# One head of an output projection loaded by three DMA engines, and the last value tile loaded in two halves

## The chip, the cores and the metric

The kernel runs on one core of a Trainium2 chip. The metric is the device time of one execution in microseconds (us). A kernel was run several times, and its median is quoted. The experiments were sent in four calls. Each call ran on one chip, with its own runs of the kernel before on that chip; different calls had different chips.

## The reference

Decode attention for 32 sequences with one query each: 32 query heads share 8 key/value heads of 128 elements, and only the last 512 cache positions count. Then comes a projection with wo.

```python
W = min(4096, max(256, Sk // 4))                                # 512
q = (x @ wq).reshape(B, Sq, Hq, Dh).transpose(0, 2, 1, 3)
k = jnp.repeat(k_cache[:, :, Sk - W:, :], rep, axis=1)
v = jnp.repeat(v_cache[:, :, Sk - W:, :], rep, axis=1)
p = softmax(jnp.einsum("bhqd,bhkd->bhqk", q, k) * Dh ** -0.5)
o = jnp.einsum("bhqk,bhkd->bhqd", p, v)
return o.transpose(0, 2, 1, 3).reshape(B, Sq, Hq * Dh) @ wo     # wo: 4096 x 512
```

## The kernel before

All loads but the 32 KB of x go out on one queue, issued by SyncE: keys and values in 2 MB tiles (128 partitions, 16 KB each), wq, and at the end wo. The last value tile, V15, is one load. Then wo follows in eight head groups of 512 KB (128 partitions with rows of 4 KB); the last group is split into 3 KB and 1 KB per partition, so that only a quarter of it has to be waited for last.

```python
# SyncE: the values, then wo
sp.dma_start(V_sb[:, n % NV:n % NV + k].rearrange("p a r d -> p (a r d)"), cache_rows(v_cache, n, k)
).then_inc(sem_v[n % NV], 16)
...
sp.wait_ge(pe_PV, 2 * Z_HOME.rindex("w") + 2)
for hg in range(NHG):
    for i0, i1 in ((0, 4),) if hg < NHG - 1 else ((0, WO_CUT), (WO_CUT, 4)):
        sp.dma_start(
            wo_sb[:, hg, i0:i1].rearrange("p i n -> p (i n)"),
            wo[hg * 512:(hg + 1) * 512, :].rearrange("(m i) n -> m (i n)", i=4)[:, i0 * 512:i1 * 512],
        ).then_inc(sem_last if i0 else sem_wo[hg], 16)
```

TensorE multiplies each value tile in 64 matmuls. Then it reorders the attention output with a band matrix (`select`: partition m of group g must hold rows 4m to 4m + 3 of wo's group), and projects.

```python
def pv(m):                       # waits for sem_v, then 64 matmuls into O_ps
    ...
for hg in range(NHG):
    pe.wait_ge(sem_wo[hg], 16)
    for i in range(4):
        if hg == NHG - 1 and i == WO_CUT:
            pe.wait_ge(sem_last, 16)
        for c in range(2):
            ins = pe.matmul(X_ps[32 * c:32 * (c + 1), 2, 0:256], lhsT=o_sel[:, i, hg, :],
                            rhs=wo_sb[:, hg, i, c * 256:(c + 1) * 256], ...)
ins.then_inc(pe_fin, 1)
```

Of the kernel before, what the change touches and what calls it, by code (L numbers as in the profile page):

```python
# [12 lines left out]
def bass_standalone__sliding_block_cached__sampling_kernel(  # L13
# [32 lines left out]
    WO_CUT = 3  # L46
# [25 lines left out]
    with ExitStack() as es:  # L72
# [13 lines left out]
        mask = sb("mask", [P, NBG], F32)  # L86
        oT_sb = sb("oT_sb", [P, HQ, B], BF16)
# [9 lines left out]
        o_sel = K_0[:, 0:HQ * B].rearrange("p (i g b) -> p i g b", i=4, g=NHG)  # L97
        band = K_0[:, HQ * B:HQ * B + 4 * 224].rearrange("p (i n) -> p i n", i=4)
# [24 lines left out]
        sem_wo = [sem(f"sem_wo{i}") for i in range(NHG)]  # L123
        sem_last = sem("sem_last")
# [33 lines left out]
        pool_qbd = sem("pool_qbd")  # L158
        nc.scalar.dma_start(x_sb, x.rearrange("b s d -> b (s d)")).then_inc(sem_x, 16)
# [27 lines left out]

        def cache_rows(cache, m, k=1):
            q, e = divmod(m, 2)
            rows = cache[4 * q:4 * q + 4, :, SK - W:, :].rearrange("b g (s r) d -> (b g) s (r d)", s=KS)  # L190
            return rows[:, :, e * CR * DH:(e + k) * CR * DH]

        @block.sync
        def _(sp):
            for name in DMA_ORDER:
# [5 lines left out]
                elif name[0] == "K":  # L201
                    if n >= NK:
                        sp.wait_ge(dve_T, 2 * (n - NK + 1))
                    sp.dma_start(
                        K_sb[:, n % NK].rearrange("p r d -> p (r d)"), cache_rows(k_cache, n)
                    ).then_inc(sem_k[n % NK], 16)
                else:
                    k = 2 if n in V_PAIRED else 1
                    if n + k > NV:
                        sp.wait_ge(pe_PV, n - NV + k)  # L210
                    sp.dma_start(
                        V_sb[:, n % NV:n % NV + k].rearrange("p a r d -> p (a r d)"), cache_rows(v_cache, n, k)
                    ).then_inc(sem_v[n % NV], 16)
            sp.wait_ge(pe_PV, 2 * Z_HOME.rindex("w") + 2)
            for hg in range(NHG):
                for i0, i1 in ((0, 4),) if hg < NHG - 1 else ((0, WO_CUT), (WO_CUT, 4)):
                    sp.dma_start(  # L217
                        wo_sb[:, hg, i0:i1].rearrange("p i n -> p (i n)"),
                        wo[hg * 512:(hg + 1) * 512, :].rearrange("(m i) n -> m (i n)", i=4)[:, i0 * 512:i1 * 512],
                    ).then_inc(sem_last if i0 else sem_wo[hg], 16)  # L220
# [8 lines left out]
        def _(pool):  # L229
# [48 lines left out]
            pool.wait_ge(pool_band, 1)  # L278
# [3 lines left out]
            ).then_inc(pool_band, 1)  # L282

        @block.tensor
        def _(pe):
# [64 lines left out]
            def pv(m):  # L350
# [9 lines left out]
                for r in range(CR):  # L360
                    ins = pe.matmul(  # L361
# [7 lines left out]
            def select(b0, b1, dst):  # L369
# [3 lines left out]
                for i in range(4):  # L373
                    for hi in range(4):
# [3 lines left out]
                            rhs=oT_sb[:, :, b0:b1].rearrange("p (g hi) b -> p hi g b", hi=4)[:, hi],  # L378
                            start=(hi == 0), stop=(hi == 3), tile_position=(0, 0), skip_group_check=True,
                        )  # L380
                ins.then_inc(pe_sel, 1)

            for name in PE_ORDER:
                k = int(name[1:])
                {"S": scores, "P": p_turn, "V": pv}[name[0]](k)
                if name == "V12":
                    pe.wait_ge(pool_band, 2)
                    nb = SELCUT
                    select(0, nb, lambda i: X_ps[:, i // 2, (i % 2) * NHG * nb:(i % 2 + 1) * NHG * nb])
            nl = B - SELCUT  # L390
            select(SELCUT, B, lambda i: S_ps[:, i // 2, (i % 2) * NHG * nl:(i % 2 + 1) * NHG * nl])
            pe.wait_ge(dve_sel, 2)
            pe.wait_ge(act_sel, 2)
            for hg in range(NHG):
                pe.wait_ge(sem_wo[hg], 16)
                for i in range(4):
                    if hg == NHG - 1 and i == WO_CUT:
                        pe.wait_ge(sem_last, 16)
                    for c in range(2):
                        ins = pe.matmul(  # L400
                            X_ps[32 * c:32 * (c + 1), 2, 0:256],
                            lhsT=o_sel[:, i, hg, :],
                            rhs=wo_sb[:, hg, i, c * 256:(c + 1) * 256],
                            start=(hg == 0 and i == 0), stop=(hg == NHG - 1 and i == 3),
                            tile_position=(0, 32 * c),
                        )
# [3 lines left out]
        def _(dve):  # L410
# [62 lines left out]
            def sel_evac(src, i0, ni, b0, b1):  # L473
                return (
                    o_sel[:, i0:i0 + ni, :, b0:b1],
                    src[:, 0:ni * NHG * (b1 - b0)].rearrange("p (i g b) -> p i g b", i=ni, g=NHG),
# [3 lines left out]
            dve.tensor_copy(*sel_evac(X_ps[:, 0], 0, 2, 0, SELCUT)).then_inc(dve_sel, 1)  # L480
            dve.wait_ge(pe_PV, NCH)
# [5 lines left out]
            dve.tensor_copy(*sel_evac(S_ps[:, 0], 0, 2, SELCUT, B)).then_inc(dve_sel, 1)  # L487
            dve.wait_ge(pe_fin, 1)
# [3 lines left out]
        def _(act):  # L492
# [52 lines left out]
            for name in ACT_ORDER:  # L545
                arg = [int(a) for a in name[1:].split(".")]
                {"E": soften, "N": norm, "C": pt_evac, "O": o_evac, "Z": spread}[name[0]](*arg)
                if name == "Z7.3":
                    act.wait_ge(pe_sel, 1)
                    act.activation(  # L550
                        o_sel[:, 2:4, :, 0:SELCUT],
                        X_ps[:, 1, 0:2 * NHG * SELCUT].rearrange("p (i g b) -> p i g b", i=2, g=NHG),
                        ACTF.Copy,
                    ).then_inc(act_sel, 1)
            nl = B - SELCUT
            act.wait_ge(pe_sel, 2)
            act.activation(
                o_sel[:, 2:4, :, SELCUT:B],
                S_ps[:, 1, 0:2 * NHG * nl].rearrange("p (i g b) -> p i g b", i=2, g=NHG),
                ACTF.Copy,  # L560
            ).then_inc(act_sel, 1)
            act.wait_ge(pe_fin, 1)
# [29 lines left out]
```

## Time and profile before

| What | Before |
|---|---|
| time, median of the first 3 runs | 187.25 us |
| DMA queue, share of 16 engines over the span | 96.5% |
| last increment of V15's load, slowest engine | 172.57 us |
| first projection matmul | 178.41 us |
| last increment of the last wo load, slowest engine | 182.72 us |
| last matmul ends | 183.06 us |

Times inside an execution count from the start of its span. An "increment" is one of the updates that the records show on a load's semaphore as it lands. In the profile before, each load of the queue got sixteen, and I read each as one DMA engine's share having landed: over the wo loads the sixteen keep their spacing (from the first to the last 3.40 us at group 0 and 3.42 at group 6). So their times show how far the engines lie apart. They and the single packets (start, length, bytes) are records of the trace; the packets do not carry the number of their engine.

### The profile page before, as it was taken

Reading aid. Unit: us, or ns where it says so; the run is one execution under the profiler, and the core shown is the slowest. Engines: PE = TensorE matmul, PEld = TensorE weight load, DVE = VectorE, ACT = ScalarE, POOL = GpSimd, SP = SyncE. Lnnn points to the kernel's source line nnn. Section 1 sums busy time; section 2 is a strip of 40 time slices with the busy share of each in tenths; the row PEclk is TensorE's granted clock in tenths of the full one; section 3 lists DMA queues with packets and bytes.
Section 4 is the critical chain, followed back from the end, with each engine's and each line's share of the span. In section 5 each row is a group of like instructions: output and inputs, shape, how many; then the busy total and the mean of one; then the engine's idle time right before and its main releaser. Section 6 shows DMA issues by size and latency. Waiting matters only on the chain.

```text
span 185.5 us, 3711 instructions
## 1 busy us (share of the span) xinstructions
PE 109.5 (59%) x1540; PEld 90.3 (49%) x1540; DVE 132.1 (71%) x239; ACT 81.2 (44%) x141; POOL 31.8 (17%) x82
## 2 busy tenths in 40 slices
PE   0220303454469704994430899155999989998773
PEld 0100001141369403974130878014998888997761
DVE  0018699979799799979999269999999975510020
ACT  3000100129900686027941005965939999961000
POOL 7100029515300250042330015000003000000000
PEclk9999999999559965799965599755599999999999
DMA  6999999989999999999999999989999999999980
GB/s 201 428 445 424 431 421 484 445 367 424 424 421 445 413 435 421 428 435 410 458 438 392 445 410 442 463 382 442 415 431 431 410 438 417 438 410 416 400 338 30
DMA packets 5872, 75.80 MB, mean 409 GB/s; under 512 B 672, under 2 KB 864, under 8 KB 1888
## 3 DMA queue, kind: packets, MB, share of 16 engines
q1 hardware_dynamic: 5808, 75.53, 96.5%
q8 instruction: 12, 0.20, 0.4%
q10 hardware_dynamic: 48, 0.03, 0.1%
q14 instruction: 4, 0.03, 0.0%
HBM read 75.53 MB, written 0.03 MB: 407 GB/s over the span
## 4 chain that ended last, share of the span: by engine, by line
DMA 41%; PE 22%; DVE 20%; ACT 7%; issue 6%; SPq 3%
PE O_ps L361 16%; DMA V_sb<-in_v_cache_dram 11%; DMA w_sb<-in_wo_dram 11%; DVE KT_sb L439 10%; DMA K_sb<-in_k_cache_dram 10%; DMA w_sb<-in_wq_dram 9%; DVE w_sb L461 5%; PE S_ps L322 4%; ACT w_sb L530 4%; DVE QA_sb L429 2%; SPq L217 2%; ACT KT_sb L530 1%; PE PT_ps L341 1%; DVE maxv L446 1%; PE X_ps L302 1%
## 5 line engine op out<-in xcount | busy, mean ns | idle before, releaser
L439 DVE STREAM_TRANSPOSE KT_sb<-K_sb 128x2048 uint32<-128x2048 uint32 x32 | 72.5, 2290 | 12.9 <-DMA K_sb<-in_k_cache_dram 12.9
L361 PE MATMUL O_ps<-w_sb,V_sb 128*128 128x128 bf16 x640 | 45.4, 240 | 10.0 <-DVE w_sb L461 5.1
L361 PEld LDWEIGHTS O_ps<-w_sb,V_sb 128*128 128x128 bf16 x640 | 44.2, 108 | 12.0 <-issue 6.1
L271 POOL COPY QBD<-QA_sb 32x64 bf16<-32x64 bf16 x64 | 25.5, 539 | 83.0 <-PE S_ps L322 60.5
L530 ACT ACTIVATE w_sb<-PTc,mask 128x512 bf16<-128x512 bf16 x60 | 38.7, 725 | 0.0
L461 DVE TENSOR_SCALAR w_sb<-PTc,mask 128x512 bf16<-128x512 bf16 x100 | 31.1, 379 | 2.3 <-ACT PTc L521 1.1
L322 PE MATMUL S_ps<-KT_sb,QBD 128*32 128x512 bf16 x256 | 20.2, 465 | 18.2 <-POOL QBD L271 11.0
L341 PE MATMUL PT_ps<-P_bf,pick 128*128 128x128 bf16 x128 | 12.6, 277 | 24.6 <-ACT P_bf L511 20.0
L341 PEld LDWEIGHTS PT_ps<-P_bf,pick 128*128 128x128 bf16 x128 | 10.9, 128 | 28.2 <-ACT P_bf L511 22.8
L502 ACT ACTIVATE X_ps<-S_ps,negmax 128x512 f32<-128x512 f32 x8 | 5.2, 649 | 39.5 <-DVE negmax L448 39.5
L322 PEld LDWEIGHTS S_ps<-KT_sb,QBD 128*32 128x32 bf16 x256 | 7.5, 108 | 27.7 <-POOL QBD L271 11.9
L361 PE MATMUL O_ps<-K_sb,V_sb 128*128 128x128 bf16 x256 | 15.1, 217 | 2.3 <-DMA V_sb<-in_v_cache_dram 2.3
L530 ACT ACTIVATE K_sb<-PTc,mask 128x512 bf16<-128x512 bf16 x24 | 15.3, 717 | 1.6 <-DVE KT_sb L439 1.6
L361 PEld LDWEIGHTS O_ps<-K_sb,V_sb 128*128 128x128 bf16 x256 | 14.5, 96 | 3.1 <-issue 3.1
L540 ACT ACTIVATE oT_sb<-O_ps 128x128 bf16<-128x128 f32 x7 | 5.2, 742 | 16.9 <-PE O_ps L361 16.9
L461 DVE TENSOR_SCALAR K_sb<-PTc,mask 128x512 bf16<-128x512 bf16 x40 | 10.7, 346 | 2.4 <-ACT PTc L521 2.4
L302 PE MATMUL X_ps<-w_sb,oT_sb 128*32 128x512 bf16 x32 | 3.8, 627 | 10.6 <-DMA w_sb<-in_wq_dram 10.6
L482 DVE CAST oT_sb<-O_ps 128x128 bf16<-128x128 f32 x1 | 0.7, 711 | 12.9 <-PE O_ps L361 12.9
L496 ACT ACTIVATE KT_sb<-X_ps 128x512 bf16<-128x512 f32 x1 | 0.6, 597 | 17.3 <-PE X_ps L302 17.3
L511 ACT ACTIVATE P_bf<-X_ps,recip 128x512 bf16<-128x512 f32 x8 | 5.5, 682 | 6.0 <-DVE recip L454 6.0
L530 ACT ACTIVATE KT_sb<-PTc,mask 128x512 bf16<-128x512 bf16 x12 | 8.0, 726 | 0.0
L361 PE MATMUL O_ps<-KT_sb,V_sb 128*128 128x128 bf16 x128 | 7.5, 217 | 0.7 <-DMA V_sb<-in_v_cache_dram 0.7
(43 smaller groups left out, 56.0 us busy)
## 6 DMA issues: line engine op xcount, KB each, us to landing
K_sb<-in_k_cache_dram SPq DMA_DIRECT2D x16, 2048.0 KB, 15.0
V_sb<-in_v_cache_dram SPq DMA_DIRECT2D x10, 2048.0 KB, 15.4
V_sb<-in_v_cache_dram SPq DMA_DIRECT2D x3, 4096.0 KB, 23.4
w_sb<-in_wq_dram SPq DMA_DIRECT2D x2, 2048.0 KB, 11.8
w_sb<-in_wo_dram SPq DMA_DIRECT2D x7, 512.0 KB, 18.2
w_sb<-in_wo_dram SPq DMA_DIRECT2D x1, 384.0 KB, 21.0
w_sb<-in_wo_dram SPq DMA_DIRECT2D x1, 128.0 KB, 17.5
oT_sb<-in_x_dram ACTq DMA_DIRECT2D x1, 32.0 KB, 4.4
```

Of the source, the lines that this page charges most:

```text
L217: sp.dma_start(wo_sb[:, hg, i0:i1].rearrange("p i n -> p (i n)"), wo[hg * 512:(hg + 1) * 512, :].rearrange("(m i) n -> m (i n)", i=4)[:, i ...
L271: pool.tensor_copy(dst[:, i, :, x0:x0 + 4], src).then_inc(pool_qbd, 1)
L302: ins = pe.matmul(X_ps[32 * c:32 * c + 32, k, :], lhsT=xT_sb[:, kt, :], rhs=w_sb[:, kt, c * 1024 + k * 512:c * 1024 + (k + 1) * 512], star ...
L322: ins = pe.matmul(S_ps[32 * c:32 * c + 32, q % 2, :], lhsT=QBD[:, q % 2, g, b, e, :], rhs=bass.AP(tensor=KT_sb, offset=s0 * slot + (b * G ...
L341: ins = pe.matmul(PT_ps[:, r, :], lhsT=pick[:, r, KS - s:KS - s + P], rhs=P_bf[:, s, :], start=(s == 0), stop=(s == KS - 1), tile_position ...
L361: ins = pe.matmul(O_ps[:, q % 2, 0:P], lhsT=V_sb[:, m % NV, r, :], rhs=z_of(q)[:, :, x0 + r, :], start=(e == 0 and r == 0), stop=(e == 1 a ...
L439: dve.transpose(KT_w[:, n % NK, b].rearrange("p i r s -> p r i s"), K_w[:, n % NK, :, 32 * b:32 * b + 32],).then_inc(dve_T, 1)
L461: ins = dve.tensor_scalar(z_of(q)[:, k].rearrange("p x r -> p (x r)"), PTc[:, q % RING].rearrange("p x r -> p (x r)"), mask[:, k:k + 1], N ...
L502: act.activation(P_f32, S_ps[:, q % 2, :], ACTF.Exp, bias=negmax[:, q:q + 1], scale=SCALE, accum_out=sums[:, q:q + 1],).then_inc(act_exp, 1)
L511: act.activation(P_bf[:, :, :], P_f32.rearrange("p (x s) -> p s x", s=KS), ACTF.Copy, scale=recip[:, q:q + 1],).then_inc(act_P, 1)
L530: ins = act.activation(z_of(q)[:, k].rearrange("p x r -> p (x r)"), PTc[:, q % RING].rearrange("p x r -> p (x r)"), ACTF.Copy, scale=mask[ ...
L540: act.activation(oT_sb[:, :, 4 * q:4 * q + 4].rearrange("p h a -> p a h"), O_ps[:, q % 2, 0:P].rearrange("p (a h) -> p a h", a=4), ACTF.Co ...
```

## The change

The intent is to take work from the DMA engines that finish last and give it to engines that finish early. A load of three rows was expected to run on three engines. So head 28 of wo (128 KB) is cut into sixteen rows of 8 KB: four loads of three rows, and one of four rows. The other three heads of the last group are loaded in 1 KB rows and projected without reordering. Because TensorE has more to do, V15 is loaded in two halves and its first half is multiplied early.

```diff
-    WO_CUT = 3
+    NG = NHG - 1
+    H0 = 4 * NG
+    FEW = (slice(0, 9, 4), slice(1, 10, 4), slice(2, 11, 4), slice(3, 12, 4), slice(12, 16, 1))
 ...
+                    if n < NCH - 1:
+                        sp.dma_start(dst, src).then_inc(sem_v[n % NV], 16)
+                    else:
+                        cut = CR * DH // 2
+                        sp.dma_start(dst[:, 0:cut], src[:, :, 0:cut]).then_inc(sem_v[n % NV], 16)
+                        sp.dma_start(dst[:, cut:], src[:, :, cut:]).then_inc(sem_half, 16)
 ...
+            for parts in FEW:
+                n = len(range(16)[parts])
+                row = H0 * DH + 8 * first
+                sp.dma_start(
+                    few_w[parts].rearrange("p i n -> p (i n)"),
+                    wo[row:row + 8 * n, :].rearrange("(m i) n -> m (i n)", i=8),
+                ).then_inc(sem_few, 16)
+                first += n
+            for hg in range(NG):
+                sp.dma_start(wo_sb[:, hg]..., wo[hg * 512:(hg + 1) * 512, :]...).then_inc(sem_wo[hg], 16)
+            sp.dma_start(wo_sb[:, NG, 1:3], ...two heads, 1 KB rows...).then_inc(sem_wo[NG], 16)
+            sp.dma_start(wo_sb[:, NG, 3], wo[(H0 + 3) * DH:, :]).then_inc(sem_last, 16)
 ...
+                    if m == NCH - 1 and r == CR // 2:
+                        pe.wait_ge(sem_half, 16)
 ...
+                if hg == NG - 2:
+                    pe.wait_ge(sem_few, 16 * len(FEW))
+                    for i in range(8):
+                        project(few_o[:, i, :], few_w[:, i], False, False)
```

Left out: a wait of SyncE for VectorE's last transposes before the rows (they go into the memory of a key tile), eight small selection matmuls per `select`, four small copies on VectorE and ScalarE, and a memset and five selects on GpSimd that build the band for the loaded head.

More of the change, by code (lines that the diff above doesn't have):

```diff
@@ L86, in bass_standalone__sliding_block_cached__sampling_kernel @@
         mask = sb("mask", [P, NBG], F32)
+        few_o = sb("few_o", [16, 8, B], BF16)
         oT_sb = sb("oT_sb", [P, HQ, B], BF16)
@@ L97, in bass_standalone__sliding_block_cached__sampling_kernel @@
         o_sel = K_0[:, 0:HQ * B].rearrange("p (i g b) -> p i g b", i=4, g=NHG)
+        few_w = K_0[0:16, 4096:8192].rearrange("p (i n) -> p i n", i=8)
+        few_band = K_0[:, HQ * B + 4 * 224:HQ * B + 4 * 224 + 128].rearrange("p (i m) -> p i m", i=8)
         band = K_0[:, HQ * B:HQ * B + 4 * 224].rearrange("p (i n) -> p i n", i=4)
@@ L123, in bass_standalone__sliding_block_cached__sampling_kernel @@
         sem_wo = [sem(f"sem_wo{i}") for i in range(NHG)]
+        sem_few = sem("sem_few")
+        sem_half = sem("sem_half")
         sem_last = sem("sem_last")
@@ L158, in bass_standalone__sliding_block_cached__sampling_kernel @@
         pool_qbd = sem("pool_qbd")
+        dve_few = sem("dve_few")
+        act_few = sem("act_few")
         nc.scalar.dma_start(x_sb, x.rearrange("b s d -> b (s d)")).then_inc(sem_x, 16)
@@ L186, in z_waits, with few_evac @@
                 eng.wait_ge(pe_S, NQUAD)
+        def few_evac(src, i0, b0, b1):
+            n0 = 2 * NG * (b1 - b0)
+            return (
+                few_o[:, i0:i0 + 4, b0:b1],
+                src[:, n0:n0 + 4 * (b1 - b0)].rearrange("p (i b) -> p i b", i=4),
+            )
         def cache_rows(cache, m, k=1):
@@ L210, in _ @@
                         sp.wait_ge(pe_PV, n - NV + k)
-                    sp.dma_start(
-                        V_sb[:, n % NV:n % NV + k].rearrange("p a r d -> p (a r d)"), cache_rows(v_cache, n, k)
-                    ).then_inc(sem_v[n % NV], 16)
-            sp.wait_ge(pe_PV, 2 * Z_HOME.rindex("w") + 2)
-            for hg in range(NHG):
-                for i0, i1 in ((0, 4),) if hg < NHG - 1 else ((0, WO_CUT), (WO_CUT, 4)):
-                    sp.dma_start(
-                        wo_sb[:, hg, i0:i1].rearrange("p i n -> p (i n)"),
-                        wo[hg * 512:(hg + 1) * 512, :].rearrange("(m i) n -> m (i n)", i=4)[:, i0 * 512:i1 * 512],
-                    ).then_inc(sem_last if i0 else sem_wo[hg], 16)
+                    dst = V_sb[:, n % NV:n % NV + k].rearrange("p a r d -> p (a r d)")
+                    src = cache_rows(v_cache, n, k)
+                    if n < NCH - 1:
[4 more added lines that the diff above has]
+                        sp.dma_start(dst[:, cut:], src[:, :, cut:]).then_inc(sem_half, 16)
+            sp.wait_ge(pe_PV, 2 * Z_HOME.rindex("w") + 2)
+            sp.wait_ge(dve_T, 2 * NCH)
+            first = 0
+            for parts in FEW:
[7 more added lines that the diff above has]
+            for hg in range(NG):
+                sp.dma_start(
+                    wo_sb[:, hg].rearrange("p i n -> p (i n)"),
+                    wo[hg * 512:(hg + 1) * 512, :].rearrange("(m i) n -> m (i n)", i=4),
+                ).then_inc(sem_wo[hg], 16)
+            sp.dma_start(
+                wo_sb[:, NG, 1:3], wo[(H0 + 1) * DH:(H0 + 3) * DH, :].rearrange("(h d) n -> d h n", h=2)
+            ).then_inc(sem_wo[NG], 16)
+            sp.dma_start(wo_sb[:, NG, 3], wo[(H0 + 3) * DH:, :]).then_inc(sem_last, 16)
             sp.wait_ge(dve_out, 1)
@@ L277, in _ @@
             pool.memset(band[:, :, :], 0.0).then_inc(pool_band, 1)
-            pool.wait_ge(pool_band, 1)
+            pool.memset(few_band[:, :, :], 0.0).then_inc(pool_band, 1)
+            pool.wait_ge(pool_band, 2)
             pool.affine_select(
@@ L282, in _ @@
             ).then_inc(pool_band, 1)
+            first = 0
+            for parts in FEW:
+                n = len(range(16)[parts])
+                spots = few_band[:, :, parts]
+                pool.affine_select(
+                    out=spots, in_=spots, compare_op=ALU.not_equal, fill=1.0,
+                    base=-8 * first, pattern=[[-1, 8], [-8, n]], channel_multiplier=1,
+                ).then_inc(pool_band, 1)
+                first += n
         @block.tensor
@@ L367, in pv, with few_at, select @@
                 ins.then_inc(pe_PV, 1)
-            def select(b0, b1, dst):
+            def few_at(ps, nb):
+                n0 = 2 * NG * nb
+                return lambda i: ps[0:16, i // 4, n0 + (i % 4) * nb:n0 + (i % 4 + 1) * nb]
+            def select(b0, b1, dst, few):
                 pe.wait_ge(act_O, min(b1 // 4, NQUAD - 1))
@@ L377, in select @@
                             lhsT=band[:, i, 96 - 32 * hi:224 - 32 * hi],
-                            rhs=oT_sb[:, :, b0:b1].rearrange("p (g hi) b -> p hi g b", hi=4)[:, hi],
+                            rhs=oT_sb[:, 0:H0, b0:b1].rearrange("p (g hi) b -> p hi g b", hi=4)[:, hi],
                             start=(hi == 0), stop=(hi == 3), tile_position=(0, 0), skip_group_check=True,
                         )
+                for i in range(8):
+                    ins = pe.matmul(
+                        few(i),
+                        lhsT=few_band[:, i],
+                        rhs=oT_sb[:, H0, b0:b1],
+                        start=True, stop=True, tile_position=(0, 0), skip_group_check=True,
+                    )
                 ins.then_inc(pe_sel, 1)
@@ L386, in _ @@
                 if name == "V12":
-                    pe.wait_ge(pool_band, 2)
+                    pe.wait_ge(pool_band, 3 + len(FEW))
                     nb = SELCUT
-                    select(0, nb, lambda i: X_ps[:, i // 2, (i % 2) * NHG * nb:(i % 2 + 1) * NHG * nb])
+                    select(
+                        0, nb, lambda i: X_ps[:, i // 2, (i % 2) * NG * nb:(i % 2 + 1) * NG * nb], few_at(X_ps, nb)
+                    )
             nl = B - SELCUT
-            select(SELCUT, B, lambda i: S_ps[:, i // 2, (i % 2) * NHG * nl:(i % 2 + 1) * NHG * nl])
+            select(
+                SELCUT, B, lambda i: S_ps[:, i // 2, (i % 2) * NG * nl:(i % 2 + 1) * NG * nl], few_at(S_ps, nl)
+            )
@@ L392, in _, with project @@
             pe.wait_ge(dve_sel, 2)
             pe.wait_ge(act_sel, 2)
-            for hg in range(NHG):
+            def project(lhsT, rhs, start, stop):
+                for c in range(2):
+                    ins = pe.matmul(
+                        X_ps[32 * c:32 * (c + 1), 2, 0:256],
+                        lhsT=lhsT, rhs=rhs[:, c * 256:(c + 1) * 256],
+                        start=start, stop=stop, tile_position=(0, 32 * c),
+                    )
+                return ins
+            for hg in range(NG):
@@ L395, in _ @@
                 pe.wait_ge(sem_wo[hg], 16)
                 for i in range(4):
-                    if hg == NHG - 1 and i == WO_CUT:
-                        pe.wait_ge(sem_last, 16)
-                    for c in range(2):
-                        ins = pe.matmul(
-                            X_ps[32 * c:32 * (c + 1), 2, 0:256],
-                            lhsT=o_sel[:, i, hg, :],
-                            rhs=wo_sb[:, hg, i, c * 256:(c + 1) * 256],
-                            start=(hg == 0 and i == 0), stop=(hg == NHG - 1 and i == 3),
-                            tile_position=(0, 32 * c),
-                        )
+                    project(o_sel[:, i, hg, :], wo_sb[:, hg, i], hg + i == 0, False)
@@ L407, in _ @@
+                if hg == NG - 2:
+                    pe.wait_ge(dve_few, 2)
+                    pe.wait_ge(act_few, 2)
+                    pe.wait_ge(sem_few, 16 * len(FEW))
+                    for i in range(8):
+                        project(few_o[:, i, :], few_w[:, i], False, False)
+            for i in range(1, 4):
+                pe.wait_ge(sem_last if i == 3 else sem_wo[NG], 16)
+                ins = project(oT_sb[:, H0 + i, :], wo_sb[:, NG, i], False, i == 3)
             ins.then_inc(pe_fin, 1)
@@ L474, in sel_evac @@
                 return (
-                    o_sel[:, i0:i0 + ni, :, b0:b1],
-                    src[:, 0:ni * NHG * (b1 - b0)].rearrange("p (i g b) -> p i g b", i=ni, g=NHG),
+                    o_sel[:, i0:i0 + ni, 0:NG, b0:b1],
+                    src[:, 0:ni * NG * (b1 - b0)].rearrange("p (i g b) -> p i g b", i=ni, g=NG),
                 )
@@ L480, in _ @@
             dve.tensor_copy(*sel_evac(X_ps[:, 0], 0, 2, 0, SELCUT)).then_inc(dve_sel, 1)
+            dve.tensor_copy(*few_evac(X_ps[0:16, 0], 0, 0, SELCUT)).then_inc(dve_few, 1)
             dve.wait_ge(pe_PV, NCH)
@@ L487, in _ @@
             dve.tensor_copy(*sel_evac(S_ps[:, 0], 0, 2, SELCUT, B)).then_inc(dve_sel, 1)
+            dve.tensor_copy(*few_evac(S_ps[0:16, 0], 0, SELCUT, B)).then_inc(dve_few, 1)
             dve.wait_ge(pe_fin, 1)
@@ L550, in _ @@
                     act.activation(
-                        o_sel[:, 2:4, :, 0:SELCUT],
-                        X_ps[:, 1, 0:2 * NHG * SELCUT].rearrange("p (i g b) -> p i g b", i=2, g=NHG),
+                        o_sel[:, 2:4, 0:NG, 0:SELCUT],
+                        X_ps[:, 1, 0:2 * NG * SELCUT].rearrange("p (i g b) -> p i g b", i=2, g=NG),
                         ACTF.Copy,
                     ).then_inc(act_sel, 1)
+                    act.activation(*few_evac(X_ps[0:16, 1], 4, 0, SELCUT), ACTF.Copy).then_inc(act_few, 1)
             nl = B - SELCUT
@@ L557, in _ @@
             act.activation(
-                o_sel[:, 2:4, :, SELCUT:B],
-                S_ps[:, 1, 0:2 * NHG * nl].rearrange("p (i g b) -> p i g b", i=2, g=NHG),
+                o_sel[:, 2:4, 0:NG, SELCUT:B],
+                S_ps[:, 1, 0:2 * NG * nl].rearrange("p (i g b) -> p i g b", i=2, g=NG),
                 ACTF.Copy,
             ).then_inc(act_sel, 1)
+            act.activation(*few_evac(S_ps[0:16, 1], 4, SELCUT, B), ACTF.Copy).then_inc(act_few, 1)
             act.wait_ge(pe_fin, 1)
```

## The prediction

Passages that told of the hardware what no trace of this case shows are cut, and the cuts are marked. No term of the sum is among them: it stands as -0.23 + 0.05 + 0 = about -0.17 us, which gave 187.1 us. "Engines 0 to 2" and "engine 3" are my names for the three engines of a three-row load and the fourth that a four-row load adds; "from 4 up" are the other twelve. No record carries such a number, and in the profile before every load of the queue left sixteen increments, so that few rows run on few engines, and the same ones each time, was an assumption when this was written. "Engines 0 to 7" and "0 to 4" in the expectations further down are names of the same kind, for the engines of loads of eight and of five rows.

> **What bounds the kernel now.** I read the slices first, then the DMA queues, the chain of waits, the windows over the last 8 us, and last the trace's own packet records and semaphore landings. The slices and queues, from the page:
>
> ```profile
> DMA  6999999989999999999999999989999999999980
> GB/s 201 428 445 424 431 421 484 445 367 424 424 421 445 413 435 421 428 435 410 458 438 392 445 410 442 463 382 442 415 431 431 410 438 417 438 410 416 400 338 30
> ...
> q1 hardware_dynamic: 5808, 75.53, 96.5%
> q8 instruction: 12, 0.20, 0.4%
> ```
>
> The 16 DMA engines are busy from the second slice to the last but one. 75.53 MB on one queue take 96.5% of the span, so what ends the kernel is the moment at which the last byte lands, plus a short tail. The chain of waits (start, length, what) says the same for the end:
>
> ```profile
> 157.89 0.59 SPq L217
> ...
> 161.37 21.03 DMA w_sb<-in_wo_dram
> 182.40 0.04 issue
> 182.45 0.63 PE X_ps L400 x8
> 183.08 0.02 issue
> 183.10 0.41 DVE oT_sb L489
> ```
>
> The reader is to see that the wo loads are issued from 157.89 us on and land at 182.40: they stand in a queue behind the last values, so their issue is not the limit, the draining is. The engine view (start, length, work, and the idle time before it) shows how close TensorE is behind:
>
> ```profile
> 172.70 3.77 PE L361 MATMUL O_ps<-K_sb,V_sb 128*128 128x128 bf16 x64 [1.17 <-DMA V_sb<-in_v_cache_dram]
> ...
> 178.41 2.80 PE L400 MATMUL X_ps<-w_sb,K_sb 128*32 128x256 bf16 x48 [0.41 <-DVE K_sb L487]
> 181.51 0.61 PE L400 MATMUL X_ps<-w_sb,K_sb 128*32 128x256 bf16 x8 [0.30 <-DMA w_sb<-in_wo_dram]
> 182.45 0.61 PE L400 MATMUL X_ps<-w_sb,K_sb 128*32 128x256 bf16 x8 [0.33 <-DMA w_sb<-in_wo_dram]
> ```
>
> TensorE does six head groups of the projection in 2.80 us (48 matmuls, 58 ns apart), then waits twice for wo, 0.30 and 0.33 us. It has caught up, with about 0.6 us to spare. The windows table (stretch, its length, busy time of the engines, clock, DMA share, GB/s) shows how the loading ends:
>
> ```profile
> 178.00:179.00 1.00, 0.59 (x12) 0.62 (x14) 0.29 (x1) 0.28 (x1) 0.00 (x0) 1.00 1.01 394
> 179.00:180.00 1.00, 1.00 (x24) 1.00 (x20) 0.00 (x0) 0.00 (x0) 0.00 (x0) 1.00 0.69 270
> 180.00:180.50 0.50, 0.50 (x15) 0.50 (x12) 0.00 (x0) 0.00 (x0) 0.00 (x0) 1.00 0.52 201
> 180.50:181.00 0.50, 0.50 (x14) 0.42 (x8) 0.00 (x0) 0.00 (x0) 0.00 (x0) 1.00 0.46 156
> 181.00:181.50 0.50, 0.20 (x4) 0.00 (x0) 0.00 (x0) 0.00 (x0) 0.00 (x0) 1.00 0.20 80
> 181.50:182.00 0.50, 0.49 (x8) 0.32 (x8) 0.00 (x0) 0.00 (x0) 0.00 (x0) 1.00 0.18 70
> 182.00:182.50 0.50, 0.17 (x6) 0.06 (x4) 0.00 (x0) 0.00 (x0) 0.00 (x0) 1.00 0.10 35
> ```
>
> The DMA share falls from 1.01 to 0.69, 0.46, 0.20 and 0.18 over three microseconds: the engines do not finish together. 0.18 of 16 is three engines. The share left after 179.0 adds up to 0.69 + 0.26 + 0.23 + 0.10 + 0.09 + 0.05 = 1.42 us, so perfect levelling would end the loads near 180.4 rather than 182.3. About 2 us is there to be had, in principle.
>
> **Which engines are late, and why.** Each load's semaphore gets sixteen increments, one per engine. For the last wo load they land at 179.38, four at 179.56 to 179.68, two at 180.10, six between 180.90 and 181.38, three at 182.66 to 182.72. The same groups can be followed back: at 12.8 us all sixteen lie within 0.37 us, and one engine at a time then drops back by about 1.45 us. Each drop follows one of the twelve 16,384-byte packets of the instruction queue (44.3, 61.5, 79.2 ... 162.6, 171.5, 180.8 us; 1.0 to 1.1 us long). Between two of them TensorE has run about 250 instructions. The ninth (154.0 us), tenth and eleventh hit engines that had been hit already, which makes the three laggards at +3.3 us; six engines have about one drop, seven have none or a small one (four 8,192-byte packets). The twelfth, at 180.82, came when its engine had nothing left to load.
>
> [...] 1 KB takes 46 ns, 3 KB 121, 4 KB 159, 16 KB 613, that is 46 down to 38 ns per KB. [...]
>
> **The change part by part.** (1) Bytes moved between engines. Before, each engine carries per load of 512 KB eight 4 KB packets and a 9 ns increment: 8 x 159 + 9 = 1,281 ns. Seven of them, plus 8 x 121 + 9 = 977 and 8 x 46 + 9 = 377, give 10.32 us of wo. After, an engine from 4 up carries the seven, two heads of 1 KB rows (16 x 46 + 9 = 745) and one (377): 10.09 us, or 0.23 less. Engine 3 gets one 8 KB row on top, engines 0 to 2 five. Taking 8 KB as 307 ns (my estimate between 159 for 4 KB and 613 for 16 KB), that is 5 x 316 = 1.58 us, so engines 0 to 2 end 1.35 us later than now and engine 3 0.09 later. (2) The last value tile in halves: 16 packets of 8 KB and two increments against 8 of 16 KB and one, 16 x 307 + 18 against 8 x 613 + 9: 0.02 to 0.06 us more on every engine. (3) So the laggards, if they are not engines 0 to 2, end 0.23 - 0.05 = 0.18 us earlier, near 182.54 instead of 182.72. (4) Tail. Before, six of the last eight matmuls fit between 182.40 and 182.72 and two follow: end at 183.06, 0.34 after the last landing. After, heads 1 and 2 land 0.35 us before head 3, four matmuls fit between, two follow: 0.34 again. No gain. (5) TensorE. Added are 8 + 8 small selections and 14 projection matmuls (16 for the loaded head, 6 for the other three, instead of 8 of group seven): 30 at 58 ns, 1.7 us. Against it, half of the last tile is multiplied before the other half lands: the half should land about 2.4 us sooner, before V14's matmuls end at 171.53, so V15 ends near 175.3 instead of 176.5. The first projection matmul then starts near 177.3 instead of 178.4, waits for groups 3 to 5, and after group 5 (landing near 180.25) runs 8 + 16 matmuls until 181.65, while group 6 lands at 181.5 and its 8 end at 182.1, just before the last rows. It fits, with some 0.2 us to spare, so (5) is off the path. (6) VectorE and ScalarE each get two copies of 0.3 us, needed only after group 5; VectorE idles 12.88 us before that. GpSimd gets a memset and five selects near 139 to 145 us, needed at 161.5. (7) SyncE issues six more loads, 0.43 to 0.6 us each, from 157.3 us on; the leading engine finishes the values at 169.13, so this is hidden. Its queue already blocks (issues of 3.85 and 4.26 us) with no hole in the DMA share.
>
> Sum: -0.23 + 0.05 + 0 = about -0.17 us on the end of the loads, and the same on the time: 187.25 - 0.17 = 187.1 us.
>
> **The rivals.** (A) Engines 0 to 2 are the laggards. The packet records carry no engine number, so the trace cannot exclude it. Then they end 1.35 us later and the time is 188.6 us. Against it: the change gives five rows to each of three engines and one to the fourth, which looks chosen for engines known to be early; seven of 16 are early. I give it one in seven. (B) The twelfth instruction block comes earlier. Some 35 more TensorE instructions stand ahead of it, and V15 ends sooner, so it moves from 180.8 to about 179, when its engine still has wo to load. That engine, now one drop behind (+1.6 to +2.0), becomes a fourth laggard at +3.0 to +3.4: the same as the other three. Cost 0 to 0.2 us, time 187.1 to 187.3. [...] (C) TensorE becomes the bound through the 30 matmuls, if the halves bring less than 1.1 us: then up to 0.5 us lost, 187.4 to 187.6. The 1.17 us wait before V15 speaks against it. (D) The levelling gives all of the 2 us: 185.3 us. Against it, nothing is taken from the three laggards except 8 KB each; they set the end.
>
> **Range and chances.** The main path and (B) give 187.0 to 187.3, (C) up to 187.6, an 8 KB packet or a tail that does better 186.8. I take 187.1, with 186.8 to 187.6. Two per cent is 3.7 us, more than any rival makes: even (A) is 0.7% and (D) 1.1%. So within 2% gets 0.98, faster 0.01, slower 0.01.
>
> **What would show it.** In the profile after: the DMA share still falls in steps, with three or four engines busy to about 182.1; the loads' increments of engines 4 up come 0.18 us earlier; three engines that ended near 179.4 now end near 180.8; TensorE's last wait is still for wo and its last two matmuls end 0.34 us after the last landing; V15's second half starts with no wait; the last instruction packet is near 179 us. I am wrong if the laggards' last landing moves by over 0.5 us in either direction, if TensorE's last idle is for something other than wo, or if an idle hole appears in the DMA share between 160 and 179 us.

## The result, and the profile after

| | Before | After |
|---|---|---|
| median (runs) | 187.29 us (4) | 187.03 us (4) |
| range | 187.17 to 187.41 | 186.97 to 187.19 |
| ratio, 95% interval | | 0.9988, 0.997 to 1.0005 |
| last increment of V15 | 172.57 | 172.76 |
| first projection matmul | 178.41 | 177.35 |
| last increment of wo | 182.72 | 182.65 |
| last matmul ends | 183.06 | 183.00 |

A ratio is the mean time of one kernel's runs over that of the other's of the same rounds, so it is not quite the ratio of the medians. The interval includes 1. The execution with the profile, 187.19 us, was the slowest of the four.

The page's slices of the DMA engines, and two of its queues (packets, MB, share of 16 engines):

```profile
DMA  6999999989999999999998999999999999999991
...
q1 hardware_dynamic: 6112, 75.53, 96.7%
q8 instruction: 12, 0.20, 0.4%
```

The bytes and the share are as before, and there are again twelve instruction packets. The windows over the end (stretch, length, busy time of PE, PEld, DVE, ACT, POOL, clock, DMA share, GB/s):

```profile
178.00:179.00 1.00, 1.00 (x24) 0.99 (x19) 0.00 (x0) 0.00 (x0) 0.00 (x0) 1.00 1.04 400
179.00:180.00 1.00, 0.83 (x14) 0.32 (x8) 0.00 (x0) 0.00 (x0) 0.00 (x0) 1.00 0.78 303
180.00:180.50 0.50, 0.03 (x2) 0.04 (x4) 0.00 (x0) 0.00 (x0) 0.00 (x0) 1.00 0.79 297
180.50:181.00 0.50, 0.50 (x8) 0.28 (x8) 0.00 (x0) 0.00 (x0) 0.00 (x0) 1.00 0.60 215
181.00:181.50 0.50, 0.50 (x12) 0.44 (x12) 0.00 (x0) 0.00 (x0) 0.00 (x0) 1.00 0.37 129
181.50:182.00 0.50, 0.50 (x14) 0.26 (x9) 0.00 (x0) 0.00 (x0) 0.00 (x0) 1.00 0.29 100
182.00:182.50 0.50, 0.50 (x12) 0.38 (x12) 0.00 (x0) 0.00 (x0) 0.00 (x0) 1.00 0.07 23
```

The reader is to see that the fall is later: at 180.00 the share is 0.79 where it was 0.52. It then ends in the same place. The early engines were filled up; the last ones moved little. TensorE's view (start, length, work, idle before it):

```profile
167.83 7.37 PE L407 MATMUL O_ps<-K_sb,V_sb 128*128 128x128 bf16 x128 [0.89 <-DMA V_sb<-in_v_cache_dram]
...
177.35 2.48 PE L458 MATMUL X_ps<-w_sb,K_sb 128*32 128x256 bf16 x40 [0.40 <-DVE K_sb L559]
...
180.47 0.61 PE L458 MATMUL X_ps<-w_sb,K_sb 128*32 128x256 bf16 x8 [0.64 <-DMA w_sb<-in_wo_dram]
...
181.01 1.04 PE L458 MATMUL X_ps<-K_sb,few_o 16*32 16x256 bf16 x16
...
181.99 0.61 PE L458 MATMUL X_ps<-w_sb,K_sb 128*32 128x256 bf16 x8
...
182.43 0.55 PE L458 MATMUL X_ps<-w_sb,oT_sb 128*32 128x256 bf16 x6
182.70 0.10 PEld L458 LDWEIGHTS X_ps<-w_sb,oT_sb 128*32 128x32 bf16 x2 [0.16 <-DMA w_sb<-in_wo_dram]
```

V14 and V15 now run as one block of 128 matmuls, with no wait for the second half. The projection starts 1.06 us earlier. But from 180.47 on TensorE hardly stops: its only wait after that is 0.16 us, before the last two matmuls. The chain that ended last says it in another way:

```profile
180.42 0.04 issue
180.47 2.54 PE X_ps L458 x38
183.00 0.02 issue
183.03 0.41 DVE oT_sb L562
```

The chain now takes TensorE from 180.47 to the end; before, it took the wo load until 182.40. Loads and TensorE end within 0.16 us of each other.

**What the increments show.** Behind the first increment of the same load, the sixteen of the last wo load came at 0, four at 0.18 to 0.30, two at 0.72, six at 1.5 to 2.0, and three at 3.3 us before. After, they came at 0, three at 0.16 to 0.31, six at 1.39 to 1.87, then 2.33, 2.52, 2.94, and three at 3.06 to 3.14. The row loads' own sixteen increments let me match them: the three engines with five rows each (the prediction's 0 to 2) were one of the earliest and two some 0.7 us behind, and they now end among the six at 1.39 to 1.87, at 2.33 and at 2.52. The one at 2.94 fits only the engine with one row (its engine 3), the last of the middle group: it was 2.15 us behind when V15's first half had landed.

### The profile page after: what moved, and what is told of

It is laid out like the page before. It is cut to its first block, busy times and chain, and to the rows that moved or that the text cites. A ratio compares the mean times of both kernels' runs of the same rounds, so it can differ in the third digit from the quotient of the medians.

```text
span 185.4 us, 3794 instructions
## 1 busy us (share of the span) xinstructions
PE 110.2 (59%) x1570; PEld 90.3 (49%) x1570; DVE 133.0 (72%) x241; ACT 81.6 (44%) x143; POOL 33.2 (18%) x88
## 4 chain that ended last, share of the span: by engine, by line
DMA 38%; DVE 24%; PE 21%; ACT 6%; SPq 5%; issue 5%; DVEq 0%
PE O_ps L407 15%; DVE KT_sb L510 13%; DMA V_sb<-in_v_cache_dram 11%; DMA K_sb<-in_k_cache_dram 10%; DMA w_sb<-in_wo_dram 9%; DMA w_sb<-in_wq_dram 9%; DVE w_sb L532 6%; ACT w_sb L603 4%; DVE QA_sb L500 2%; PE S_ps L366 2%; SPq L241 2%; SPq L247 2%; ACT KT_sb L603 1%; PE X_ps L458 1%; DVE maxv L517 1%
## 5 line engine op out<-in xcount | busy, mean ns | idle before, releaser
L532 DVE TENSOR_SCALAR w_sb<-PTc,mask 128x512 bf16<-128x512 bf16 x100 | 31.9, 387 | 2.6 <-PE O_ps L407 1.3
L385 PE MATMUL PT_ps<-P_bf,pick 128*128 128x128 bf16 x128 | 11.8, 265 | 24.1 <-ACT P_bf L584 19.4
L385 PEld LDWEIGHTS PT_ps<-P_bf,pick 128*128 128x128 bf16 x128 | 10.1, 122 | 27.9 <-ACT P_bf L584 22.5
L532 DVE TENSOR_SCALAR K_sb<-PTc,mask 128x512 bf16<-128x512 bf16 x40 | 10.7, 344 | 2.4 <-ACT PTc L594 2.4
L407 PEld LDWEIGHTS O_ps<-KT_sb,V_sb 128*128 128x128 bf16 x128 | 7.2, 96 | 2.4 <-issue 2.3
```

What stands on the lines that cost most here:

```text
L385: ins = pe.matmul(PT_ps[:, r, :], lhsT=pick[:, r, KS - s:KS - s + P], rhs=P_bf[:, s, :], start=(s == 0), stop=(s == KS - 1), tile_position ...
L407: ins = pe.matmul(O_ps[:, q % 2, 0:P], lhsT=V_sb[:, m % NV, r, :], rhs=z_of(q)[:, :, x0 + r, :], start=(e == 0 and r == 0), stop=(e == 1 a ...
L532: ins = dve.tensor_scalar(z_of(q)[:, k].rearrange("p x r -> p (x r)"), PTc[:, q % RING].rearrange("p x r -> p (x r)"), mask[:, k:k + 1], N ...
```

## The experiments

**e1_halves_only.** The kernel before, with V15 in two halves and nothing else.

```diff
-sp.dma_start(V_sb[:, n % NV:n % NV + k]..., cache_rows(v_cache, n, k)).then_inc(sem_v[n % NV], 16)
+if n < NCH - 1: sp.dma_start(dst, src).then_inc(sem_v[n % NV], 16)
+else:           # two loads of half the columns, the second on sem_half
+                    if m == NCH - 1 and r == CR // 2:
+                        pe.wait_ge(sem_half, 16)
```

> Only the last value tile in two halves; wo as in the kernel before. Main theory (the three latest DMA engines set the end, TensorE does not): the loads end 0.05 to 0.2 us later through the smaller packets (182.8 to 182.9 against 182.72 us), V15's matmuls end about 1.2 us sooner, and the time is 187.3 to 187.5 us, not better than before. Rival (the TensorE chain after the last values is what the change shortens): 0.2 us or more faster than before, 187.0 or less.

Measured: 187.44 us (187.03 to 187.64) against 187.23, ratio 1.0002 (0.999 to 1.0015). V14 and V15 ran without a gap, the projection started at 177.50, and TensorE then waited three times for wo, 0.62, 0.64 and 0.35 us. So an earlier TensorE is worth nothing by itself. The rival falls. The loads ended at 183.20, later than the 182.8 to 182.9 that I expected; but the latest engine was already 0.42 us later than in the profile before when V14 had landed (168.06 against 167.64), so the halves did not do that. V15 itself took 4.97 us on the slowest engine against 4.93.

**e2_rows_only.** The changed kernel with V15 in one load.

```diff
-                    if n < NCH - 1: ...
-                    else: ...two halves...
+                    sp.dma_start(dst, src).then_inc(sem_v[n % NV], 16)
-                    if m == NCH - 1 and r == CR // 2:
-                        pe.wait_ge(sem_half, 16)
```

> The whole change but for the halves: last value tile in one load. Main theory: the loads end 0.23 us sooner than before (182.5), but TensorE, with 30 more matmuls and a start of the projection at 178.4 or later, becomes the bound: first projection matmul near 178.8, 78 matmuls of 58 ns, end near 183.2, so 187.2 to 187.5 us and no wait of TensorE for the last wo load. Rival (TensorE never matters, only the loads): last matmul 0.34 us after the last landing, 187.0 us or less.

Measured: 187.93 us (187.58 to 188.29), ratio 1.0032 (1.002 to 1.0045), slower than I expected. The chain that ended last and TensorE's view:

```profile
179.46 4.66 PE X_ps L450 x78
```

```profile
179.46 2.80 PE L450 MATMUL X_ps<-w_sb,K_sb 128*32 128x256 bf16 x48 [0.40 <-DVE K_sb L551]
182.19 1.04 PE L450 MATMUL X_ps<-K_sb,few_o 16*32 16x256 bf16 x16
183.16 0.61 PE L450 MATMUL X_ps<-w_sb,K_sb 128*32 128x256 bf16 x8
183.61 0.49 PE L450 MATMUL X_ps<-w_sb,oT_sb 128*32 128x256 bf16 x6
```

All 78 matmuls run in one piece, with no wait for any wo load: TensorE is the bound. The rows need the halves. In this execution V15 landed late, at 173.42, its latest engine 4.27 us behind the first (3.43 before); the engines lay 1.08 us apart already after the first half of wq (0.36 in the profile before). TensorE ends 10.7 us after V15 lands here, so with the 172.57 of before it would have ended near 183.3, 0.2 us later than before; this last is an estimate from those numbers. The last wo load landed at 183.25, not at the 182.5 that I expected.

**e3_rows_on_8.** The changed kernel, with the sixteen rows in two loads of eight.

```diff
-    FEW = (slice(0, 9, 4), slice(1, 10, 4), slice(2, 11, 4), slice(3, 12, 4), slice(12, 16, 1))
+    FEW = (slice(0, 16, 2), slice(1, 16, 2))
```

> The changed kernel, but the sixteen 8 KB rows in two loads of 8 rows[...]. Main theory: the latest engines are none of 0 to 7 and lose the same 8 KB as in the changed kernel, so the last landing is the same within 0.1 us (182.65) and the time 187.0 to 187.15 us; the sixteen increments of the row loads (eight per load) all land within about 1.9 us of the first, none 3 us late. Rival (some of the engines 0 to 7 are among the three latest): one to three increments come over 3 us after the first, and the end is 0.25 us later than in the changed kernel, 187.3 us.

Measured: 188.51 us (187.91 to 189.26), ratio 1.0067 (1.0049 to 1.0084). Both theories missed it: I expected 187.0 to 187.3. The 8 KB packets between 169.2 and 174 us took 414 ns at the median (314 in the changed kernel), the 4 KB packets of other loads were slower in the same microseconds (193 ns in the mean against 162 before), and the last wo load landed at 183.41 instead of 182.65. The increments of the rows, sixteen in all as in e6, lay 3.9 us apart, not 1.9. On top of that the granted clock fell:

```profile
182.00:183.00 1.00, 1.00 (x18) 0.63 (x16) 0.00 (x0) 0.00 (x0) 0.00 (x0) 0.79 0.28 86
183.00:184.00 1.00, 1.00 (x12) 0.61 (x8) 0.00 (x0) 0.00 (x0) 0.00 (x0) 0.50 0.00 0
```

The column before the DMA share is the clock: 0.79, then 0.50, where the changed kernel has 1.00 up to its end. The last fourteen matmuls took from 182.58 to 184.26, about 0.7 us more than the same fourteen after the change (181.99 to 182.98). In the profiles before and after, a drop to 0.5 also comes, but at 186.1 and 184.3 us, when TensorE is done. Why it came at 182.6 here was not tested.

**e6_own_ports.** The same two loads of eight rows, to other partitions: four apart over 0 to 29 instead of two apart over 0 to 15. The guess was that e3's rows get into each other's way where they are written; the run's name comes from it. The runs show what the partitions did to the packets, not by what means.

```diff
-    FEW = (slice(0, 16, 2), slice(1, 16, 2))
+    FEW = (slice(0, 32, 4), slice(1, 32, 4))
+    NF = 32        # few_w, few_o and the band over 32 partitions; the unused ones meet zeros
```

> As e3_rows_on_8 (sixteen 8 KB rows, two each on engines 0 to 7), but written to partitions 0, 4, ... 28 and 1, 5, ... 29 instead of 0 to 15[...]. Theory of the collision: the 8 KB packets after 169 us go back from 370 to 440 ns to under 330 ns, the leading engine is no longer held up, no clock drop falls into the projection, and the time is 187.0 to 187.3 us, 1.2 us under e3. Rival (eight row loads are slow by themselves, or engines 0 to 7 include the latest ones): packets stay above 370 ns or increments come 3 us after the first, and the time stays over 188 us.

Measured: 187.05 us (186.85 to 187.63), ratio 1.0 (0.9987 to 1.0014). The 8 KB packets took 313 ns (at most 324; 414 in e3), the last load landed at 182.56, and the clock stayed at 1.00. Against the kernel before, the same rows in loads of the same size cost 0.67% or 1.25 us less than in e3; in the profiles 0.85 us of the difference are the loads (183.41 against 182.56) and the rest is mostly the clock. In the loads only the partitions differ, so where the rows are written is what slowed e3's packets; that much is shown. In this execution, the eight engines with rows were 0 to 2.33 us behind when the values had landed, and the two latest engines, at 3.44 and 3.57, were not among them.

**e5_fewer_pe.** The kernel before with every second value matmul of tiles 0 to 11 left out. The result is wrong (relative error 0.59). In the profile before, 194 to 326 TensorE records lay between two of the 16,384-byte instruction packets, 259 in the mean; 768 instructions fewer are about three packets at that rate, an estimate from these numbers.

```diff
-                for r in range(CR):
+                step = 2 if m < 12 else 1
+                for r in range(0, CR, step):
```

> The kernel before with half of the value matmuls of tiles 0 to 11 left out (wrong result on purpose): 768 fewer TensorE instructions, the same bytes in the same order. Main theory [...]: nine 16 KB instruction packets instead of twelve, the ninth near the end, so no engine is held up twice while it still loads; the last wo landing comes 1.2 to 1.5 us earlier and the time is 185.8 to 186.2 us. Rival (the engines differ for another reason, fetches only coincide with it): three engines still land near 182.7 and the time stays at 187.2 us.

Measured: 186.33 us (186.11, 186.16, 186.49 and 187.37), ratio 0.9961 (0.994 to 0.9982). The queue and the last windows:

```profile
q8 instruction: 9, 0.15, 0.3%
```

```profile
180.00:181.00 1.00, 0.68 (x14) 0.39 (x10) 0.00 (x0) 0.00 (x0) 0.00 (x0) 1.00 0.48 183
181.00:182.00 1.00, 0.68 (x14) 0.35 (x10) 0.00 (x0) 0.00 (x0) 0.00 (x0) 1.00 0.11 31
182.00:183.00 1.00, 0.36 (x8) 0.10 (x2) 0.41 (x1) 0.38 (x1) 0.00 (x0) 1.00 0.00 0
```

There are nine instruction packets (twelve before), and no engine is more than 2.45 us behind the first at the end; the group at 3.3 us is gone. The last wo load landed at 182.02 against 182.72, while the first engine ended 0.2 us later than before (179.58 against 179.38), so it is the spread that shrank. With the bytes the same, fewer instructions, and three packets of them fewer, made the loads end 0.70 us earlier. In the profile before, the group of the latest engines grew from one to two to three (landings at 162.71; 167.59 and 167.64; 173.77 to 173.81) after the packets of 153.96, 162.60 and 171.49. Together this says that these packets set how late the last engines are. The gain is 0.7 us and not my 1.2 to 1.5, because the latest engine that was left was still 2.45 us behind. By the increments it stood at 1.6 us after one 16 KB packet and went to 2.5 at 133.6 us, when another 16 KB packet and one of the four 8,192-byte instruction packets came 0.07 us apart. The execution of 187.37 has no profile, and I can't explain it.

**c_after_again and c_after_third.** The changed kernel unaltered, as a yardstick. They were run at other times.

```diff
 (no edit)
```

> The changed kernel once more, on the chip of this call, as the yardstick for the next three runs: 187.0 to 187.3 us, ratio to the kernel before 0.997 to 1.000.

> The changed kernel as the yardstick on this call's chip: 186.9 to 187.2 us, no execution near 188.4 (which would be five rows on an engine hit twice); n4_five_engines 0.2 to 0.4 us below it.

Measured: 187.09 us (186.87 to 187.20) against 187.18, ratio 0.9993 (0.9981 to 1.0005); and 187.13 us (186.93 to 187.22) against 187.24, ratio 0.9992 (0.998 to 1.0004). With the first result, the differences of the means are 0.23, 0.13 and 0.14 us. Each interval includes 1, but the sign is the same three times. None of the 14 executions was over 187.22 us.

**n1_lower8 and n2_12of16.** Can the idea be taken further? These two start from the kernel before and load 64 (n1) or 96 (n2) of the 128 partitions of the last head group in loads of eight rows of 4 KB, and the rest in one load.

```diff
+            for p0 in EIGHTS:                       # n1: 0-3, 32-35; n2: also 64-67
+                rows = slice(p0, p0 + 29, 4)
+                sp.dma_start(wo_sb[rows, NHG - 1]..., wo_rows[NHG - 1][rows]).then_inc(sem_low, 16)
+            sp.dma_start(wo_sb[REST:, NHG - 1]..., wo_rows[NHG - 1][REST:]).then_inc(sem_wo[NHG - 1], 16)
```

> A version of my own: the kernel before, one value tile in one load, but the lower 64 partitions of the last head group of wo in eight loads of 8 rows of 4 KB [...], first in the queue, its matmuls first, and the 3 KB and 1 KB split on the group that now comes last. The latest engines carry 4 rows of 4 KB less (4 x 163 = 0.65 us), engines 0 to 7 4 rows more. Main theory (the latest three are not among 0 to 7): last landing 0.65 us earlier, TensorE done 0.34 us after it, 186.5 to 186.8 us. Rival (TensorE bound, or engines 0 to 7 late): 187.2 us or more.

> The same with 96 partitions in twelve loads of 8 rows: the latest engines carry 6 rows less (0.98 us), engines 0 to 7 six more[...]. Main theory: 186.2 to 186.7 us if no engine of 0 to 7 was more than 1.6 us behind; TensorE then starts to matter, because 64 matmuls from 178.4 us end at 182.1. [...]

Measured: 189.18 us, ratio 1.0105 (1.0089 to 1.012), and 189.85 us, ratio 1.0132 (1.0115 to 1.0149). Both main theories missed by over 2 us. In n1, 4 KB packets between 169.2 and 174 us took 254 ns at the median against 159 before, and the 16 KB packets of the value tile that was still coming in took 720 against 615. So V15 reached TensorE late:

```profile
173.59 3.77 PE L373 MATMUL O_ps<-K_sb,V_sb 128*128 128x128 bf16 x64 [2.41 <-DMA V_sb<-in_v_cache_dram]
```

The wait is 2.41 us where it was 1.17. Which of its loads makes the packets slow was not tested by itself. In n2 the granted clock also fell to 0.5 from 174.8 to 178.2 us, and V15's matmuls took 5.38 us instead of 3.77, so its time is not made by the packets alone.

**e7_strided.** n1 differs from e6 in another thing: the eight rows of one load lie 16 KB apart in memory. This run gives e6 that spacing.

```diff
-wo[row:row + 8 * n, :].rearrange("(m i) n -> m (i n)", i=8)
+wo[H0 * DH:(H0 + 1) * DH, :].rearrange("(m k i) n -> k m (i n)", k=2, i=8)[first // 8]
```

> e6_own_ports with one thing changed: each of its two loads of eight 8 KB rows takes every second row of 128 KB (16 KB apart, as in n1_lower8) instead of 64 KB in one piece. If the spacing of the rows in memory is what made the packets of n1_lower8 slow, the 8 KB packets after 169 us rise from 314 ns to 400 ns or more and the time to over 187.4 us. Rival (the load of 64 upper partitions, or the many loads, made them slow there): packets near 314 ns, 187.0 to 187.2 us, as e6.

Measured: the 8 KB packets took 314 ns (at most 324), as in e6, so the spacing does not slow them. The time, 187.58 us (187.35 to 187.75), was nevertheless not the 187.0 to 187.2 of the rival. In its profile one of the latest engines was 4.1 us behind from the first wo group on, against 3.5 in e6. Whether the spacing or the run has to do with it stays open.

**n3_two_heads.** From e6: two heads in 8 KB rows, in four loads of eight, their matmuls moved to where TensorE waits.

```diff
-    FEW = (slice(0, 32, 4), slice(1, 32, 4))
+    FEW = tuple(slice(j, 32, 4) for j in range(4))
-                if hg == NG - 2:
+                if hg == 2:
-            for i in range(1, 4):
+            for i in range(2, 4):
```

> A version of my own from e6_own_ports: two heads of wo instead of one in 8 KB rows on engines 0 to 7 (four loads of eight rows, partitions 0 to 31[...], each load from 64 KB in one piece), their matmuls moved from after head group 5 to after group 2, where TensorE waits anyway; two heads left in 1 KB rows. The latest engines lose another head (8 x 46 + 9 = 0.38 us) and TensorE has 2 fewer matmuls after group 5 lands, besides the 16 moved. Main theory: last landing 182.2 instead of 182.55, TensorE done 0.34 us later, 186.6 to 186.85 us, the fastest so far. Rivals: an engine of 0 to 7 that was 2.3 us behind becomes the last (then 186.8 to 187.0), or the longer selection before the projection (8 more small matmuls, 0.3 us) makes TensorE the bound (187.0 or more).

Measured: four executions at 186.72, 186.74, 186.78 and 186.82 us, as the main theory had it, and two at 187.67 and 187.87; median 186.80, ratio 0.9988 (0.997 to 1.0007). The profile fell on the 187.67:

```profile
182.54 0.61 PE L458 MATMUL X_ps<-w_sb,K_sb 128*32 128x256 bf16 x8 [0.64 <-DMA w_sb<-in_wo_dram]
182.99 0.50 PE L458 MATMUL X_ps<-w_sb,oT_sb 128*32 128x256 bf16 x4
```

TensorE waits for wo until 182.54. When the values landed, two engines were 3.05 and 3.06 us behind, and the row loads' increments show that both were among the engines with rows: their last rows landed at 173.61 and 173.62, 3.07 us after the first engine was done with its rows (170.54), so they got four more rows on top of their delay. Packets were not slow (312 ns). So which engines are 3 us behind is not the same in every execution: in e6 none of the eight with rows was (2.33 us at most), here two were. Which packets set these two back was not looked at.

**n4_five_engines.** As n3, with the rows in six loads of five and one of two, meant for five engines alone.

```diff
-    FEW = tuple(slice(j, 32, 4) for j in range(4))
+    FEW = tuple(slice(j, j + 20, 4) for j in (0, 1, 2, 3, 32, 33)) + (slice(34, 42, 4),)
```

> n3_two_heads with its two heads' rows on engines 0 to 4 alone (six loads of five rows and one of two[...]), because n3 had two executions of six near 187.8 us[...]. In every execution with a profile so far the five earliest engines of 0 to 7 were at most 0.95 us behind the leader; they now carry 6 or 7 rows (1.9 to 2.2 us) less 0.71 of the heads: +1.2 to +1.5. The latest lose the same two heads as in n3. Main theory: no execution over 187.1, median 186.65 to 186.85 us, clearly faster than the kernel before (ratio 0.997 to 0.9985). Rival (the two slow executions of n3 had another cause): again some near 187.8.

Measured: 187.33 us (187.12 to 188.03), ratio 1.0011 (0.9998 to 1.0025). My premise was wrong: in its profile one of the engines with rows was 2.09 us behind when the values had landed, and with six rows it became the last, 3.9 us behind. I had taken these five to be the earliest five of n3's eight, which no record says. No version of mine beats the changed kernel clearly.

## Why the prediction was right or wrong

The median of 187.03 us lies in the range and 0.07 from the number. By its steps:

- **The bound.** Right. e1 frees TensorE earlier and gains nothing; e5 has nine instruction packets instead of twelve and the loads end 0.7 us sooner (182.02 against 182.72).
- **(1), the laggards' bytes.** Right in size. From the landing of group 6 to the last landing, on the slowest engine, it was 1.26 us before (181.46 to 182.72) and 0.99 after (181.66 to 182.65): 0.27 less, against 0.23. The three engines with five rows filled up by about the 1.58 us of the sum (a packet of 8 KB took 313 ns at the median, estimated at 307), but two of them started some 0.7 us behind and ended at 181.84 and 182.03, not near 180.8. **Engine 3** was mis-sized: its one row was to put it 0.32 us further behind the first engine, and it went from 2.15 to 2.94, a fourth laggard. Its last value packet took 515 ns and its row, right after it, 821 (313 is usual); in the two later profiles of the changed kernel the same pair took 515 and 759, and 448 and 616 ns. The prediction has no term for where rows are written: the last row load puts its four rows on four neighbouring partitions, 12 to 15. In e6, with the rows of each load four partitions apart, no 8 KB packet took over 324 ns, with an instruction packet in the same microseconds. That this is what slowed e3's packets too is my guess, not shown; the changed kernel with only those four rows moved was not run.
- **(2), the halves.** Right, 0.02 to 0.06 us predicted, but V15 lost more than that: it took 4.93 us on the slowest engine before (167.64 to 172.57) and 5.07 after (167.69 to 172.76), 0.14 more. In the later profiles of the changed kernel it took 5.06 and 5.10. With the same halves and no rows (e1), or with every load's rows four partitions apart (e6, e7, n3, n4, the last with six or seven rows meant for each of five engines), it took 4.97 to 4.99. So the halves cost about 0.05 us, and the other 0.1 goes with the way the change places its rows, which no step of the prediction counts.
- **(3), the sum for the loads.** In the two profiles the last landing moved by 0.07 us, not 0.18: the 0.27 less the 0.14, and 0.05 that V14 was late by already. These two executions took 187.18 and 187.19 us. The mean time fell by 0.13 to 0.23 us, so the predicted 0.17 is about right for the mean, though no single interval excludes zero. As the sum lacks the 0.1 us of (2), that the number came out so well is partly luck.
- **(4), the tail.** Right: 0.34 before, 0.35 after (182.65 to 183.00).
- **(5), TensorE.** Right, and narrower than I thought: 0.16 us to spare, predicted 0.2. V15 ended at 175.20 (175.3 predicted), the projection began at 177.35 (177.3). e2 shows what (5) is worth: without the halves the changed kernel is 0.6 us slower than the kernel before. How much of that is the late V15 seen in its profile is not known.
- **(6), (7).** Right: neither the copies, GpSimd nor the issues appear as a wait, and the DMA share has no hole (0.96 or more in every 2 us from 160 to 178 us).
- **Rival (A)** did not occur: no execution of the changed kernel was near 188.6. n3 shows that with the rows on more engines such executions do occur (187.67 and 187.87 us). That the three engines with five rows are always spared is what 14 executions and three profiles say, not a rule.
- **Rival (B)** was wrong in its timing: the twelfth instruction packet came at 180.71, not near 179, and cost nothing.
- **Rival (C)** is nearly reached: with 0.16 us left, TensorE would take over at once if the loads ended sooner. **Rival (D)** did not occur, for the reason given.

## What to carry to other kernels

When sixteen DMA engines share a queue that never runs dry, look at the sixteen increments of the last load and not at the mean share: here the end was set by the latest few, and only what was taken from those counted (the share at 180.00 us rose from 0.52 to 0.79, the last landing moved by 0.07 us). Loads of few rows moved work to few engines here, but the partitions mattered: two loads of eight rows took 414 ns per 8 KB packet and 188.51 us on one set of partitions, 313 ns and 187.05 us on another. And it did not pay where these engines were late: in n3's profile two of them were 3.05 us behind and the time was 187.67 us, while four other executions came at 186.72 to 186.82. And if the engine behind the loads has only 0.16 us to spare, as TensorE here, a gain on the loads needs a gain there too.
